# Leaky ReLU in one ScalarE instruction, state @ w_in in half-height matmuls, and conversions paced by a budget

## Chip, cores and metric

The kernel runs on one core of a Trainium2 chip. The metric is the device time of one execution in microseconds. TensorE (PE) does the matmuls, ScalarE (ACT) and VectorE (DVE) the elementwise work, and the SP queue issues nearly all DMAs.

## What is computed

State attention, and behind it two feed-forward layers, all on float32 arrays:

```python
# x: (8, 8, 512, 64), state: (8, 8, 32, 64): batch, head, tokens or states, depth
scores = scale * x @ state.T;  a = softmax(scores);   xread = a @ state
scores2 = scale * state @ x.T; a2 = softmax(scores2); sread = a2 @ x
x = concatenate([xread, sread], axis=2)         # then heads side by side: (4352, 512)
h = x @ w_in                                    # (512, 2048)
x = maximum(0.01 * h, h) @ w_out                # (2048, 512)
g, v = x @ w_gate, x @ w_val                    # (512, 1536) each
out = (g * sigmoid(g) * v) @ w_out2             # (1536, 512)
```

The five weights arrive as 64-bit floating-point numbers, seen by the kernel as pairs of 32-bit integers, and are turned into float32 on the chip.

## The kernel before, in words

**Precision.** A float32 matrix product is made of three passes of a faster format: each operand is split into a high part (a cast on ACT, `split_h`) and the rest (a subtraction on DVE, `split_l`), and `passes` multiplies low x high, high x low and high x high. Small products (scores, `state @ w_in`, the reads of the tokens) are plain float32 matmuls.

**First layer.** The tokens are worked on in 8 blocks of 512 (j = 0 to 7) and a tail of 256, which holds the results of the states. As `xread = a @ state`, the product `xread @ w_in` is taken as `a @ (state @ w_in)`: `state_win` multiplies the states of one batch and two pairs of heads with the raw w_in tiles, 64 output rows for each pair, and `store_sw` evicts the result from PSUM on ACT and stores it to DRAM (56 such products; those of batch 0 are kept in SBUF). They are loaded again (`load_sw`) when their block is due. For this the states lie in `states` with zeros around them, so that the two heads of a pair give rows of their own.

A block has 16 slots (f = 0 to 15, one for 128 columns of w_in). A slot i runs `h_mm` two slots ahead (6 matmuls of 512 columns), `h_act` (ACT copies PSUM to `hs`, DVE makes `max(0.01 hs, hs)`, ACT casts the high part, DVE subtracts for the low part) and `y_mm` (12 matmuls). The last block (j = 7) also does the tail: 12 + 12 matmuls of 256 columns in each slot.

**What sets the order.** The schedule is written out by hand, and every engine executes in program order. For the start and the first block it stands in strings, `START` and `SLOT0`: "c" is one step of the conversion of layer 1's weights, "p" one product of `state @ w_in` (nothing if none is ready), "H" `h_mm`, "Y" and "Z" `y_mm`, and so on. `put` places the attention steps of later blocks into slots by a cost and a budget of 2.8 per slot.

**Conversion.** `convert` is a generator that takes a weight tile through five operations on ACT and DVE, in four steps for each tile, with three tiles in different stages; `finish2` takes pairs of converted tiles of layer 2, makes sums of quarters (the second layer uses a product scheme with seven multiplications) and splits, and stores them to DRAM. In blocks 1 to 6, `pump` and `pump_finish` advance the two generators by one step in each slot, and by one more in every fourth; in block 7 by up to six and five steps. At slot f == Y_SUMS (6) of block 7 what is left is run to the end before anything else of the slot is issued (lines 1382 to 1393), and the memory is handed on to the second layer's weights. `read_tokens` (lines 361 to 424) makes the states' attention; `read` multiplies the turned weights with the tokens into 32 output rows for each head, and `read_out` turns the result in eight 32x32 transposes on DVE.

**Second layer.** Four pairs of blocks; for each the products with w_gate and w_val (`quads`, line 708) and then the product with w_out2 (`read_out`, line 829). Behind the third pair stands the tail (lines 859 to 960): for each of 12 column tiles f, `split2` splits a loaded gate and val tile and asks for the next load, `hidden` multiplies, and the result is multiplied with w_out2. All loads go through one list (`order`), three tiles of it ahead.

Of the kernel before, what the change touches and what calls it, by code (L numbers as in the profile page):

```python
# [25 lines left out]
def kernel(  # L26
# [54 lines left out]
    FB = 4  # L81
# [9 lines left out]
    START = "spc0Scppccc0pp0cppccppcc1pccchcc1cccpcp1clcppp0phcccpcplp1pc01cpcpmcc"  # L91
    SLOT0 = [
        "DcHcpAcccpcSYLpcpZccc",
        "DcHcAcccppSYLpccpZccc",
        "DcHcpcpcAcSYLZccppp",
        "cpDccHcApSpccYLpcZcccc",
        "cpDcHccAppScYLcZpc",
        "cccDpHpccApccScpYLccZ",
        "cpcDcHAcpScccYcLZpcp",
        "ccDccHcAppSccppYcLcZ",  # L100
        "pcDcHcpcAppSYLcccZ",
        "ccpDHcAScYcpLpccZcp",
        "ccpDcHcASYcpLpccZcp",
        "pcDHccASccYLcpcZp",
        "pcDHccASccYLcppcZp",
        "cpcDcHAccSpYLccpccpZp",
        "pDcpcHccpcppAcSYLcpZp",
        "ppDpcHccppAcSYLpcZp",
# [4 lines left out]
    Y_SUMS = 6  # L113
# [4 lines left out]
    PUMPS = [1, 1, 1, 1, 1, 1, 1]  # L118
    BUDGET = 2.8
    EARLY = -5  # L120
    BUDGET0 = 2.6
# [37 lines left out]
    sw_dram = [[dram.tile([2, P, 512], F32, name=f"sw_dram{b}_{g}") for g in range(FB)] for b in range(B)]  # L159
# [71 lines left out]
    def convert(keys, room, prepare, load_next, finish=None):  # L231

        done, before, prev = None, None, None
        for key in keys + [None, None]:
            while key and not room(key):
                yield 0
            ops = None
# [9 lines left out]
            yield 1  # L247
# [3 lines left out]
            yield 1  # L251
            if prev:
                prev["join"]()
            yield 1
# [9 lines left out]
            yield 1  # L264
# [9 lines left out]
    def pump_finish(n):  # L274
        for _ in range(n):
            next(finishing[0], None)
# [84 lines left out]
    def read_tokens(b, q):  # L361
# [32 lines left out]
        def read():  # L394

            ps = v["ps"] = ps_a.tile([P, 512], F32, tag="b", name="ps_r")
            tokens = [xn.pop((b, p)) for p in pairs]
            for c in range(NC):
                for j in range(4):
                    nc.tensor.matmul(  # L400
                        ps[NS * j:NS * (j + 1), 0:D],
                        lhsT=v["et"][:, c * P + NS * j:c * P + NS * (j + 1)],
                        rhs=tokens[j // 2][:, c, D * (j % 2):D * (j % 2 + 1)],
                        start=(c == 0),
                        stop=(c == NC - 1),
                    )
            next_xn(2)

        def read_out():
            for j in range(4):  # L410
                for g in range(2):
                    d0 = D * (j % 2) + 32 * g
                    nc.vector.transpose(
                        out=x_tail[d0:d0 + 32, pairs[j // 2], b * NS:(b + 1) * NS],
                        in_=v["ps"][NS * j:NS * (j + 1), 32 * g:32 * g + 32],
                    )
# [6 lines left out]
            {"D": [read_out], "cost": 0.9},  # L423
# [17 lines left out]
    sw_staged = [0]  # L441
# [10 lines left out]
    def store_sw(b, g, q, ps):  # L452

        pool, tag, bufs = ((cv, "sw", 2), (xin, "xn", 2))[sw_staged[0] % 2]
        sw_staged[0] += 1
        t = pool.tile([P, 512], F32, tag=tag, name="sw", bufs=bufs)
        nc.scalar.copy(t, ps)
        nc.sync.dma_start(out=sw_dram[b][g][q], in_=t)
# [13 lines left out]
    def load_sw(b, g, q):  # L472
        assert (g, b, q) not in products
        t = SW_raw[b, g, q] = xin.tile([P, 512], F32, tag="sw", name="sw")
        nc.sync.dma_start(out=t, in_=sw_dram[b][g][q])
# [30 lines left out]
    def h_act(j, f):  # L506
# [8 lines left out]
        nc.scalar.copy(hs, ps[:, :n])  # L515
# [175 lines left out]
    def layer2(p2, ps2):  # L691
# [167 lines left out]
        def tail():  # L859
# [5 lines left out]
            def load2():  # L865
                key = next(loads, None)
                if not key:
                    return
# [18 lines left out]
            for _ in range(3):  # L887
                load2()
# [564 lines left out]
```

## Time and profile before

| | us |
|---|---|
| median of 3 runs | 1517.83 (1517.43 to 1518.1) |
| the profiled execution | 1516.83 |
| its span, first to last instruction | 1515.0 |
| PE busy in it | 1460.5 |
| DVE busy | 944.6 |
| ACT busy | 683.4 |

The rows below come from the profile of one execution. A group of instructions is given as line, engine, operation, output <- inputs, shape and count, then the busy time in us, the mean of one in ns, and the idle time of its engine ahead of it with what ended that. A row of the timeline gives start, length, engine, line and tiles, a count, and in brackets the idle time before it. A row by stretches gives from and to, the length, the busy time of PE, PE's weight loads (PEld), DVE, ACT and POOL with the instructions counted, the mean granted clock of PE (1.00 is 2.4 GHz, 0.50 is 1.2 GHz), the busy share of the DMA engines and GB/s.

### The profile page before, as it was taken

What the parts mean: (1) busy time and instruction counts of PE and PEld (TensorE: products, weight loads), DVE (VectorE), ACT (ScalarE), POOL (GpSimd) and SP (SyncE); (2) the same over time, 40 slices, a digit from 0 to 9 for tenths busy, and PEclk for the clock granted to TensorE, in tenths of its full rate; (3) what the DMA queues carried; (4) which work ended last, traced back from release to release, by engine and by line L of the source; (5) the groups of instructions that cost most, each with busy time, mean ns of one, the idle gap of its engine ahead of it and who ended that gap; (6) DMA issues with size and microseconds to landing.
All of it is one profiled execution on the core that took longest, in us unless ns stands there. A gap on an engine that the chain in (4) does not pass through costs nothing.

```text
span 1515.0 us, 20085 instructions
## 1 busy us (share of the span) xinstructions
PE 1460.5 (96%) x7114; PEld 1157.6 (76%) x7114; DVE 944.6 (62%) x1716; ACT 683.4 (45%) x1234; POOL 3.0 (0%) x8
## 2 busy tenths in 40 slices
PE   6999999999999999919999999999999998999999
PEld 2446777777777788818888888888888887988887
DVE  6888688887887876976444544445344554544442
ACT  6777555565555555645433333334333342433322
POOL 0000000000000000000000000000000000000000
PEclk9999999999999999959999999999999998999999
DMA  8885444444454545785568677676766387786445
GB/s 296 294 282 198 140 157 177 153 174 157 164 194 161 188 137 183 262 271 183 162 193 274 205 235 229 194 221 228 235 200 194 105 285 230 225 279 192 130 141 193
DMA packets 146164, 307.53 MB, mean 203 GB/s; under 512 B 14608, under 2 KB 35088, under 8 KB 145040
## 3 DMA queue, kind: packets, MB, share of 16 engines
q1 hardware_dynamic: 144912, 297.85, 60.1%
q10 hardware_dynamic: 1152, 8.39, 1.3%
q8 instruction: 57, 0.93, 0.3%
q14 instruction: 43, 0.35, 0.1%
HBM read 231.74 MB, written 74.45 MB: 202 GB/s over the span
## 4 chain that ended last, share of the span: by engine, by line
PE 51%; DMA 4%; DVE 3%; ACT 1%; issue 0%; SPq 0%; ACTq 0%; DVEq 0%
PE ps_x L708 17%; PE ps_o L433 17%; PE ps_s L708 9%; PE ps_a L708 4%; DMA wraw<-w_val 2%; PE ps_y L433 1%; PE ps_h L433 1%; DMA ws<-in_dram 1%; PE ps_yt L433 1%; DMA wo<-wo 1%; PE ps_t L433 0%; DVE wl L165 0%; ACT wh L162 0%; DVE two L219 0%; DVE hl L165 0%
## 5 line engine op out<-in xcount | busy, mean ns | idle before, releaser
L433 PE MATMUL ps_y<-gh,w_parts 128*128 128x512 f32 x1024 | 339.0, 391 | 0.0
L708 PE MATMUL ps_x<-yc,wq 128*128 128x512 f32 x1152 | 278.0, 389 | 0.0
L708 PEld LDWEIGHTS ps_x<-yc,wq 128*128 128x128 f32 x1152 | 216.2, 188 | 44.8
L433 PE MATMUL ps_o<-wo,zh 128*128 128x512 f32 x768 | 236.5, 389 | 0.0
L433 PEld LDWEIGHTS ps_y<-gh,w_parts 128*128 128x128 f32 x1024 | 192.4, 188 | 52.0 <-issue 8.1
L433 PE MATMUL ps_y<-gl,w_parts 128*128 128x512 f32 x512 | 199.5, 390 | 0.2 <-DVE gl L165 0.2
L433 PEld LDWEIGHTS ps_o<-wo,zh 128*128 128x128 f32 x768 | 144.2, 188 | 30.0
L433 PE MATMUL ps_o<-wo,zl 128*128 128x512 f32 x384 | 149.5, 389 | 0.5 <-DMA wo<-wo 0.5
L708 PE MATMUL ps_s<-yc,wq 128*128 128x512 f32 x576 | 146.1, 389 | 0.0
L162 ACT CAST gh<-hs 128x512 fp32r<-128x512 f32 (+1 forms) x144 | 85.9, 596 | 118.1 <-DVE hs L516 118.1
L165 DVE TENSOR_TENSOR zl<-z,zh 128x512 fp32r<-128x512 f32 x96 | 66.3, 691 | 116.0 <-ACT zh L162 116.0
L165 DVE TENSOR_TENSOR gl<-hs,gh 128x512 fp32r<-128x512 f32 (+1 forms) x144 | 95.3, 662 | 56.9 <-ACT gh L162 54.0
L708 PEld LDWEIGHTS ps_s<-yc,wq 128*128 128x128 f32 x576 | 108.1, 188 | 22.4
L162 ACT CAST zh<-z 128x512 fp32r<-128x512 f32 x96 | 59.3, 622 | 142.1 <-PE ps_o L433 142.0
L728 ACT ACTIVATE sg<-C 128x512 f32<-128x512 f32 x72 | 45.5, 632 | 158.5 <-DVE C L724 158.5
L433 PEld LDWEIGHTS ps_y<-gl,w_parts 128*128 128x128 f32 x512 | 96.2, 188 | 20.1 <-DVE gl L165 0.5
L724 DVE TENSOR_TENSOR C<-ps_s,C 128x512 f32<-128x512 f32 x48 | 33.2, 691 | 124.2 <-PE ps_s L708 124.2
L516 DVE SCALAR_TENSOR_TENSOR hs<-hs 128x512 f32<-128x512 f32 (+1 forms) x144 | 94.5, 656 | 25.9 <-ACT hs L515 24.8
L515 ACT COPY hs<-ps_h 128x512 f32<-128x512 f32 (+1 forms) x144 | 80.5, 559 | 60.3 <-PE ps_h L433 58.5
L433 PE MATMUL ps_h<-ah,swl 128*128 128x512 f32 x256 | 106.4, 416 | 0.5 <-DVE swl L165 0.5
L433 PE MATMUL ps_h<-al,swh 128*128 128x512 f32 x256 | 100.6, 393 | 0.0
L433 PE MATMUL ps_h<-ah,swh 128*128 128x512 f32 x256 | 100.4, 392 | 0.0
(126 smaller groups left out, 2009.3 us busy)
## 6 DMA issues: line engine op xcount, KB each, us to landing
wo<-wo SPq DMA_DIRECT2D x96, 512.0 KB, 4.7
wq<-quad_gate SPq DMA_DIRECT2D x168, 256.0 KB, 3.1
wq<-quad_val SPq DMA_DIRECT2D x168, 256.0 KB, 3.1
ws<-in_dram SPq DMA_DIRECT2D x68, 512.0 KB, 4.6
sw_dram<-sw SPq DMA_DIRECT2D x56, 256.0 KB, 3.1
sw<-sw_dram SPq DMA_DIRECT2D x56, 256.0 KB, 3.8
quad_gate<-hl SPq DMA_DIRECT2D x24, 512.0 KB, 3.5
quad_val<-hl SPq DMA_DIRECT2D x24, 512.0 KB, 3.4
```

Source lines behind the costliest of these rows:

```text
L162: nc.scalar.copy(dst, src)
L165: nc.vector.tensor_tensor(out=dst, in0=src, in1=hi.bitcast(F32), op=ALU.subtract)
L433: nc.tensor.matmul(ps, lhsT=w, rhs=v, start=first and n == 0, stop=last and n == len(todo) - 1)
L515: nc.scalar.copy(hs, ps[:, :n])
L516: nc.vector.scalar_tensor_tensor(out=hs, in0=hs, scalar=0.01, in1=hs, op0=ALU.mult, op1=ALU.max)
L708: nc.tensor.matmul(bank, lhsT=a, rhs=v, start=first and n == 0, stop=last and n == len(todo) - 1, skip_group_check=True,)
L724: nc.vector.tensor_tensor(out=kept[0], in0=bank, in1=kept[0], op=ALU.add)
L728: nc.scalar.activation(t[0], c, AF.Sigmoid)
```

## The change

- `h_act`: one ACT instruction, `Prelu` with alpha 0.01, reads PSUM and writes `hs`; the DVE instruction is gone.
- `state @ w_in`: `product_sw` takes one pair of heads and four batches. Each head is a matmul with 64 contraction rows (the head's depth), 4 x 32 = 128 output rows and 512 columns, its operands on its own half of the partitions and its result in a PSUM bank of its own. There are 32 such products (batch 0 is in them too), each with two evictions on ACT and two stores. `load_sw` gathers a batch's rows from them. `flat` becomes a buffer of its own. `START` and `SLOT0` have fewer "p".
- `read`: the tokens become the stationary operand and the turned weights the moving one, so that the result arrives already turned; `read_out` is one copy.
- Conversions: every step yields a cost in us, and `fill` advances both generators until a credit is used up. In blocks 1 to 6 a slot gives `min(FILL, SLOT - CHUNK - load)`, in two halves; in block 7 slots before Y_SUMS give 2.0. `convert` goes on with tiles under way when there is no room for a new one. Y_SUMS is 5, and the y sums of the first pair are paced by slot.
- The tail of layer 2: the first two gate and val tiles and the first two w_out2 tiles are loaded at its first step, and each is replaced by the one two further on.

```diff
-    Y_SUMS = 6
+    Y_SUMS = 5
-    PUMPS = [1, 1, 1, 1, 1, 1, 1]
     BUDGET = 2.8
+    BUDGET0 = 2.6
+    FILL = 1.9
+    CHUNK = 0.8
+    SLOT = 4.1
...
+        todo = list(keys)
+        while todo or before or (finish and done):
+            key = todo.pop(0) if todo and room(todo[0]) else None
+            if not (key or before or (finish and done)):
                 yield 0
+                continue
...
+    def fill(us):
+        credit[0] = min(credit[0] + us, 2.0)
+        while credit[0] > 0:
+            cost = (next(finishing[0], None) or 0) + (next(background[0], None) or 0)
+            if not cost:
+                break
+            credit[0] -= cost
...
-            for c in range(NC):
-                for j in range(4):
-                    nc.tensor.matmul(
-                        ps[NS * j:NS * (j + 1), 0:D],
-                        lhsT=v["et"][:, c * P + NS * j:c * P + NS * (j + 1)],
-                        rhs=tokens[j // 2][:, c, D * (j % 2):D * (j % 2 + 1)],
...
+            for i in range(2):
+                for c in range(NC):
+                    for e in range(2):
+                        n = c * P + NS * (2 * i + e)
+                        nc.tensor.matmul(
+                            ps[D * e:D * (e + 1), i],
+                            lhsT=tokens[i][:, c, D * e:D * (e + 1)],
+                            rhs=v["et"][:, n:n + NS],
...
-            for j in range(4):
-                for g in range(2):
-                    d0 = D * (j % 2) + 32 * g
-                    nc.vector.transpose(
...
+            nc.vector.tensor_copy(out=x_tail[:, pairs[0]:pairs[0] + 2, b * NS:(b + 1) * NS], in_=v["ps"])
...
+    def product_sw(g, p, bs, banks):
+        pool = ps_y if banks == "yy" else ps_a
+        ps = [pool.tile([P, 512], F32, tag=tag, name="ps_sw") for tag in banks]
+        for e in range(2):
+            half = slice(D * e, D * (e + 1))
+            nc.tensor.matmul(
+                ps[e], lhsT=flat[half, p, 4 * bs:4 * bs + 4, :].rearrange("d b n -> d (b n)"),
+                rhs=raw["in", g, p][half], start=True, stop=True,
+            )
+        for e in range(2):
+            pool, tag, bufs = ((cv, "sw", 2), (xin, "xn", 2))[e]
+            t = pool.tile([P, 512], F32, tag=tag, name="sw", bufs=bufs)
+            nc.scalar.copy(t, ps[e])
+            nc.sync.dma_start(out=sw_dram[bs][g][2 * p + e], in_=t)
...
-        nc.scalar.copy(hs, ps[:, :n])
-        nc.vector.scalar_tensor_tensor(out=hs, in0=hs, scalar=0.01, in1=hs, op0=ALU.mult, op1=ALU.max)
+        nc.scalar.activation(hs, ps[:, :n], AF.Prelu, alpha=0.01)
...
-            for _ in range(3):
-                load2()
+            for f in range(2):
+                for kind in ("gate", "val"):
+                    load2(kind, f)
+            for f in range(2):
+                load2("o", f)
...
-                pump(PUMPS[0])
+                room = min(FILL, SLOT - CHUNK - load.get(i, 0))
+                fill(room / 2)
                 next(parts)
-                pump_finish(1)
                 y_mm(j, f)
-                pump(f % 4 == 2)
-                pump_finish(f % 4 == 0)
+                fill(room / 2)
...
                 if f < Y_SUMS:
-                    pump_finish(5)
+                    fill(2.0)
                 elif f == Y_SUMS:
-                    while next(background[0], None) is not None or next(finishing[0], None) is not None:
-                        pump(1)
-                        pump_finish(1)
+                    drain()
...
-                    for _ in range(2):
+                    while summed[0] < min(2 * (f - Y_SUMS), f):
                         next(sums0, None)
+                        summed[0] += 1
```

## Rows read from the trace of the kernel before

**Rows 1.** The page: busy time of the engines, and PE's line of 40 slices

```profile
PE 1460.5 (96%) x7114; PEld 1157.6 (76%) x7114; DVE 944.6 (62%) x1716; ACT 683.4 (45%) x1234; POOL 3.0 (0%) x8
...
PE   6999999999999999919999999999999998999999
```

**Rows 2.** PE's waits, whole span: us in total, times, longest

```profile
PE ps_h L433 <- DVE cl L165: 32.1, 1, 32.1
...
PE ps_t L433 <- DVE wl L165: 4.9, 2, 3.0
```

**Rows 3.** Timeline of PE around 650 us, three slots and the wait

```profile
636.25 0.28 PE L433 MATMUL ps_yt<-gh,w_parts 128*128 128x256 f32 x1
...
643.23 0.28 PE L433 MATMUL ps_yt<-gh,w_parts 128*128 128x256 f32 x1
...
676.90 0.55 PE L433 MATMUL ps_h<-tailh,cl 128*128 128x256 f32 x1 [32.08 <-DVE cl L165]
...
684.96 0.28 PE L433 MATMUL ps_yt<-gh,w_parts 128*128 128x256 f32 x1
```

**Rows 4.** Busy time by stretches: first block, blocks 1 to 6, hole, tail

```profile
36.00:134.70 98.70, 97.96 (x397) 47.03 (x396) 79.66 (x149) 75.81 (x138) 0.00 (x0) 1.00 0.83 285
158.50:589.80 431.30, 431.01 (x2380) 341.76 (x2379) 348.84 (x722) 237.51 (x437) 0.53 (x1) 1.00 0.47 161
...
644.80:677.00 32.20, 0.12 (x2) 0.13 (x1) 24.47 (x46) 15.28 (x27) 0.00 (x0) 0.55 0.81 285
...
1270.40:1331.60 61.20, 55.94 (x362) 51.01 (x361) 30.65 (x60) 22.68 (x49) 0.00 (x0) 0.92 0.76 240
```

**Rows 5.** Groups of instructions in 645 to 677 us, one of sixteen

```profile
L211 ACT ACTIVATE ws<-ws 128x512 f32<-128x512 f32 x7 | 4.6, 657 | 12.1 <-DMA ws<-in_dram 12.1
```

**Rows 6.** Groups over the whole span: elementwise work, table loads

```profile
L516 DVE SCALAR_TENSOR_TENSOR hs<-hs 128x512 f32<-128x512 f32 x128 | 87.8, 686 | 22.2 <-ACT hs L515 21.1
...
L515 ACT COPY hs<-ps_h 128x512 f32<-128x512 f32 x128 | 74.7, 583 | 55.7 <-PE ps_h L433 54.0 <-ACT yst L556 1.2
...
L413 DVE STREAM_TRANSPOSE x_tail<-ps_r 32x32 f32<-32x32 f32 x128 | 27.2, 213 | 1.8
...
L728 ACT ACTIVATE sg<-ps_x 128x512 f32<-128x512 f32 x24 | 14.3, 597 | 24.7 <-PE ps_x L708 24.7
...
L1199 ACT ACT_TABLE_LOAD x1 | 1.3, 1283 | 5.3 <-DMA flat<-in_dram 5.3
L728 ACT ACT_TABLE_LOAD x1 | 1.3, 1283 | 0.0
```

**Rows 7.** Groups of the first block, 36 to 134.7 us: the products

```profile
L446 PE MATMUL ps_sw<-w_in,states 128*64 128x512 f32 x192 | 47.9, 607 | 0.2 <-ACT sw L457 0.2
...
L457 ACT COPY sw<-ps_sw 128x512 f32<-128x512 f32 x42 | 24.4, 585 | 11.1 <-PE ps_sw L446 5.3 <-issue 2.4 <-DMA sw_dram<-sw 1.1
...
L446 PEld LDWEIGHTS ps_sw<-w_in,states 128*64 128x64 f32 x192 | 11.8, 135 | 24.3 <-issue 14.0 <-ACT sw L457 5.4 <-ACT ws L211 1.8
```

**Rows 8.** Timeline of PE and PEld: two products between other matmuls; weight loads

```profile
31.27 0.14 PEld L446 LDWEIGHTS ps_sw<-w_in,states 128*64 128x64 f32 x2 [0.29 <-issue]
...
38.36 0.39 PE L433 MATMUL ps_h<-ah,swh 128*128 128x512 f32 x1
38.67 1.94 PE L446 MATMUL ps_sw<-w_in,states 128*64 128x512 f32 x8
...
40.54 0.50 PE L433 MATMUL ps_y<-gh,w_parts 128*128 128x512 f32 x1
```

**Rows 9.** Timeline of PE: one read of the tokens

```profile
177.17 0.65 PE L400 MATMUL ps_r<-xn,et 128*32 128x64 f32 x32
```

**Rows 10.** Timeline of PE in layer 2's tail, one step to the next

```profile
1293.55 0.40 PE L433 MATMUL ps_o<-wh,zl 128*128 128x512 f32 x1
...
1297.81 0.40 PE L433 MATMUL ps_o<-wh,zl 128*128 128x512 f32 x1
```

**Rows 11.** The chain that ended last: start, us, what was on it

```profile
1273.38 6.32 DMA wraw<-w_val
```

More of the change, by code (lines that the diff above doesn't have):

```diff
@@ L157 @@
     wo_dram = [dram.tile([P, 2, 2, 512], F32, name=f"wo_{f}") for f in range(HF)]
-    sw_dram = [[dram.tile([2, P, 512], F32, name=f"sw_dram{b}_{g}") for g in range(FB)] for b in range(B)]
+    sw_dram = [[dram.tile([H, P, 512], F32, name=f"sw_dram{bs}_{g}") for g in range(FB)] for bs in range(B // 4)]
     def split_h(dst, src):
@@ L272, in pump @@
             next(background[0], None)
-    def pump_finish(n):
-        for _ in range(n):
-            next(finishing[0], None)
+    credit = [0.0]
+    def fill(us):
[5 more added lines that the diff above has]
+            credit[0] -= cost
     def pump_until(key):
@@ L450, in state_win @@
         return ps
[L452 to L458, printed above, removed]
+    def product_sw(g, p, bs, banks):
[6 more added lines that the diff above has]
+                rhs=raw["in", g, p][half], start=True, stop=True,
+            )
+        for e in range(2):
[3 more added lines that the diff above has]
+            nc.sync.dma_start(out=sw_dram[bs][g][2 * p + e], in_=t)
     def sw_tiles(b, g, q):
@@ L472, in load_sw @@
     def load_sw(b, g, q):
-        assert (g, b, q) not in products
+        assert not any((g, p, b // 4) in products for p in (2 * q, 2 * q + 1))
         t = SW_raw[b, g, q] = xin.tile([P, 512], F32, tag="sw", name="sw")
-        nc.sync.dma_start(out=t, in_=sw_dram[b][g][q])
+        rows = slice(NS * (b % 4), NS * (b % 4 + 1))
+        nc.sync.dma_start(
+            out=t, in_=sw_dram[b // 4][g][4 * q:4 * q + 4, rows]
+        )
     def split_sw_h(b, g, q):
@@ L860, in tail, with load2 @@
             n = widths[B]
-            order = [(key, f) for f in range(NF2) for key in ("gate", "val", "o")]
-            loads = iter(order)
             raw2, parts2 = {}, {}
-            def load2():
-                key = next(loads, None)
-                if not key:
+            def load2(kind, f):
+                if f >= NF2:
                     return
-                kind, f = key
                 if kind == "o":
@@ L875, in load2 @@
                         nc.sync.dma_start(out=t.bitcast(F32), in_=wo_dram[f // 2][:, f % 2, m])
[L876 removed]
+                    parts2[kind, f] = (h, l), (ht, lt)
                 else:
[L878 to L879 removed]
+                    raw2[kind, f] = wtiles[0].take("wraw")
+                    nc.sync.dma_start(out=raw2[kind, f][0], in_=w2_dram[kind, f % HF][:, f // HF])
             yr = []
@@ L937, in tail @@
             split2("val", 1)
-            split2("o", 0)
             yield
@@ L1017, in finish1_h @@
         def finish1_h(key):
-            while any((KD * g + 2 * q) // 2 + NF1 // 2 == key[1] for g, _, q in products):
+            while any((KD * g + p) // 2 + NF1 // 2 == key[1] for g, p, _ in products):
                 pump_products(1)
@@ L1274, in take0, with drain @@
             return t, None
+        summed = [0]
         preparing, after = ExitStack(), ExitStack()
+        def drain():
+            while True:
+                steps = [next(g[0], None) for g in (finishing, background)]
+                if steps == [None, None]:
+                    return
         turn_over = max(before["state"][-1], before["tokens"][-1]) + 1
```

115 lines of the change are left out of this document (47 added, 68 removed).

## Prediction

> **What bounds the kernel now.** I read the page's table of busy time first: TensorE (PE) is busy 96% of the span, VectorE (DVE) 62% and ScalarE (ACT) 45% [rows 1]. The row of slices shows one hole in PE's line, the "1" at the eighteenth slice, around 650 us, and a "6" at the start. So PE sets the pace nearly everywhere, and what can be won is either matmul time on PE or one of its few waits. The table of PE's waits names them: 32.1 us, once, for a DVE result in the tail's h_mm, and 4.9 us, twice, in the second layer's tail [rows 2]. The timeline around the first shows what it costs in all. In the last block (j = 7) the tail's first y matmul of a slot comes every 6.98 us; over the slot with the wait the distance is 41.73 us, so the price is 34.75 us: 32.08 us of waiting and 2.7 us in which PE, then at a granted clock of about 0.5, runs half as fast [rows 3, 4]. The groups of instructions inside the hole say who is late: the integer weights of the second layer are still being converted on DVE and ACT (the drain at f == Y_SUMS, lines 1383 to 1385), in program order ahead of the operand PE waits for, and ACT itself sits 12.1 us for loads of them [rows 5]. In the long stretch of blocks 1 to 6 PE is busy 431.01 of 431.30 us, DVE 348.8, ACT 237.5: PE-bound, with room on the others [rows 4]. In the first block's weight-loading stretch, 36 to 134.7 us, PE is busy 97.96 of 98.70 us, but DVE 79.7, ACT 75.8 and the DMA engines 0.83 of it too [rows 4]: the tightest place of the kernel.
>
> **The drain.** This is the largest term. Today blocks 1 to 6 give each slot one step of conversion and one of finishing, plus a quarter more, whatever the slot's other load. After, each slot gives `min(1.9, 3.3 - load)` us, in costs that are those of DVE's instructions. One weight tile costs 2.22 us to convert; the 36 of them and the last step are about 82 us. Finishing costs 12 x 4.54 + 6 x 1.48 = 63.4. Together 146. Adding the room slot by slot from the planner's own costs gives 161 us in slots 16 to 111, so the work should end near slot 104, before block 7 (slot 112) begins, and the drain, now one slot earlier, finds nothing. What hides the 146 us there is DVE's and ACT's free time, 82 and 194 us, and what the change frees. It frees, on DVE, 96 scalar_tensor_tensor of 686 ns (65.9 us), since ACT does the leaky ReLU as it empties PSUM, and 16 times eight transposes of 213 ns against one copy of about 0.2 us (24 us) [rows 6]. It brings in what the drain and the slots ahead of it do now: 24.5 us of DVE in the hole and at most 66 steps of about 0.55 us before it, 61 us. So DVE goes from 348.8 to at most 320 of 431 us, 74%. ACT pays nothing to speak of: an ACTIVATE from PSUM takes 597 ns, the copy it replaces 583 [rows 6]. Saved: 34.75 us. If a third of the work were left at the drain, a third of the price would stay.
>
> The second layer's weight loads and the y sums also start a slot earlier; they had ten slots and more before, and no PE wait in [rows 2] is theirs. Nothing.
>
> **The products state @ w_in.** Today 56 products of two matmuls each (two heads, 64 output rows each, one batch), of which 42 lie in the stretch 36 to 134.7, with 6 kept ones of the same form: 192 PE records busy 47.9 us, so four records, one product, take 1.00 us, the block's start included; the 42 evictions to store them are of 585 ns [rows 7]. The timeline gives the same: two products between a matmul at 38.36 and one at 40.54, 2.18 us less 0.23 for the first matmul itself, 0.97 each [rows 8] (0.23: a slot of 6.98 us in rows 3 holds 18 matmuls of 512 columns and 24 of 256, so 30 lengths of 512). After, 32 products of two matmuls with 64 contraction rows and 128 output rows; following the order of pumps through the code, 7 fall in the start phase (12 before) and 25 in this stretch. The form is not in this trace. Lower bound: the two run side by side as the two column halves do now (two weight loads in the 0.14 us of one [rows 8]), 1.00 us: 17 us of PE saved. Upper bound: one after the other, some 0.93 us more each (half of the 1.87 us from 38.67 to 40.54 [rows 8]), 25 x 1.93 = 48 against 42: 6 us lost. I take the lower one, because its nearest row is the same array shared by two matmuls, only cut the other way.
>
> The Trainium skill (TensorE: Matmul & The Clock Gate, section Measured speedup vs the span model) gives four row tiles 3.07 times the speed of one, not four. By that share, 0.77, a product would take about 0.28 us more, an estimate from that page, and 25 of them would put the forecast some 7 us higher; no run here shows row tiles yet.
>
> What is late next? ACT's work there stays (50 evictions for 25 products, 42 before: 75.8 + 4.7 = 80 us at most; DVE loses 12 x 0.686, to 71 us). DMA writes 50 x 256 KB for 42: 0.83 x 98.7 = 82 us, some 5 more. So PE's 98.7 - 17 = 82 us meets three others at 71 to 87. I take 12 of the 17 us, since DMA at 87 us is the highest of the four sums, and keep 4 and 18 as ends (18: the start phase, too, has five products fewer).
>
> **The reads of the tokens.** Turned round: 16 per call still, but with 64-column weights and 32 columns streamed, where now one read's 32 records take 0.65 us [rows 9]. Lower bound: half the streaming, -0.2 us. Upper: the weight loads set the pace, 11.8 us for 192 of 64 columns [rows 7], 0.061 us each, 32 of them 1.97 us: +1.3. Nearer the row of the read itself, where loads hide: +0.2 us, 16 times, 3 us lost in a PE-bound stretch; ends -3 and +21.
>
> **The tail of layer 2.** The stretch 1270.4 to 1331.6 takes 61.2 us at a mean granted clock of 0.92 [rows 4]; a steady step of it takes 4.26 us [rows 10], twelve 51.1. (Such a step has six matmuls of 512 columns, 1.4 us, and 24 of 256, 2.9.) The 10.1 us between are the two waits and the half clock behind them: the gate and val tiles of f = 1 are asked for only when those of f = 0 are split, on SP behind the loads of `wo`; the val tile's load, issued at 1273.38, takes 6.32 us to land [rows 11]. After, f = 0 and 1 are loaded at the first step of the tail, far earlier, beside the y sums of the fourth pair, and the same late places fetch f = 2. That is wanted a step later: 1270.4 + 5.8 for the gate and val of f = 0 and 1 + 1.4 for the first output + 1.4 for the gate of f = 2 = 1279.0, against 1273.4 + 6.3 + 1.4 for its split = 1281.1 at worst. So a wait of 0 to 2 us may stay. 9 us saved, ends 5 and 10.
>
> **Sum.** The profiled execution took 1516.83 us (span 1515.0): 1516.83 - 34.75 - 12 - 9 + 3 = 1464.1. It lies 1.0 us under the median of the runs shown, 1517.83, so I forecast 1465.
>
> **The rivals.**
> The first block gives little back: DMA and the in-order ACT queue, both near 0.8 already [rows 4], keep the 98.7 us stretch at 94 or so. For: all four sums come within 15% of each other. Against: no PE wait there is put down to a load [rows 2]. 8 us less saved: 1473.
> The two 64-row matmuls run one after the other: no gain but 6 us lost in the first block, 18 more than forecast: 1483.
> Part of the drain stays: fill steps return nothing while a load is under way, and ACT's 12.1 us of waiting for loads [rows 5] shows that loads can set the pace. With a third left: 1477.
> Prelu does not share a table with Exp. The trace has two table loads of 1.283 us [rows 6], one of them before the first copies, and none between the Exps and the copies. Two more around each of 32 Exps would be 82 us of ACT, mostly in its free time in blocks 1 to 6, but 5 us of it on the path of the start: 1470. The Trainium skill (ScalarE: Activation LUTs, Rules for kernel authors) puts relu and max on VectorE rather than ScalarE; the float32 rows here speak otherwise, 686 ns on DVE against about 597 on ACT.
> Slower: the fills make DVE the bound of blocks 1 to 6. A filled slot holds 4.0 us of DVE by the budget (3.3 and the low half of g), against 431.3 / 96 = 4.49 us of PE. In the hole, conversions kept DVE busy only 24.5 of 32.2 us [rows 4], 1.31 us of time for each of work; if that held in the filled slots, they would take 5.2 us, and 88 of them 0.75 us more each, 66 us: 1531. It decides from 5.1 us a slot on. Against: in the hole ACT waited for loads, and DVE's mean afterwards is 74%.
>
> **How the numbers follow.** Chances: the forecast (with its ends, 1453 to 1469) 0.53; first block gives little 0.18; serial row tiles 0.11; part of the drain stays 0.10; table loads 0.03; slower 0.04; the change does not do what it says, since the slots fill no better and the products gain nothing, 0.01. The range leaves out the last three and the far ends: 1453 to 1483. A measurement of this kernel tells about 0.2%, 3 us, from no change: faster 0.95, same 0.01, slower 0.04.
>
> **What would show it.** Right: no PE wait for `cl` near 640 us, slots of 6.98 us throughout block 7, blocks 1 to 6 at 431 us or little more, the last conversion before block 7; groups of products of about 1.0 us; no wait on `wl` beyond 2 us in the tail, and a granted clock of 1.00 there. Wrong: PE waits for gl or swl in blocks 1 to 6 (the fills), products of 1.9 us (serial tiles), ACT waiting for `ws` loads in the first 130 us (DMA). The forecast itself falls if the hole moves rather than closes.

## The result, and the profile after

The changed kernel takes 1481.15 us (median of four runs, 1480.25 to 1482.51) against 1517.63 for the kernel before: a ratio of 0.9765, 95% interval 0.9748 to 0.9782. That is 36.5 us less, inside the predicted range of 1453 to 1483, but 16 us above the 1465 that was forecast and above the ends of the forecast itself, 1453 to 1469. The profiled execution took 1480.25 us, with a span of 1478.2.

Cut by stage, the spans (1515.0 and 1478.2) compare as follows. A block ends where ACT begins to copy its result out of PSUM (`yst<-ps_y`).

| stage | before, us | after, us | difference | forecast |
|---|---|---|---|---|
| start and first block (0 to the end of block 0) | 158.45 | 155.35 | -3.1 | -12 |
| blocks 1 to 6 | 431.30 | 438.28 | +7.0 | +3 |
| block 7, with the drain | 138.05 | 103.76 | -34.3 | -34.75 |
| second layer | 787.2 | 780.8 | -6.4 | -9 |

So the largest term came out to half a microsecond; the first block and the tail gave less than their share, and the reads, which make up the second row, cost more than theirs.

The page after: busy time of the engines and PE's line of slices.

```profile
PE 1450.5 (98%) x7018; PEld 1159.7 (78%) x7018; DVE 829.4 (56%) x1460; ACT 688.2 (47%) x1242; POOL 3.0 (0%) x8
...
PE   5999999999999999999999999999999999999998
```

The hole of [rows 1] is gone and only the start and the last slice are below 9. DVE has lost 115 us of work, and its last conversion of a weight ends at 588 us, before block 7 begins at 593.63; before the change it was at 675, inside block 7. The waits of PE, whole span (us in total, times, longest):

```profile
PE ps_s L319 <- ACT states L1213: 7.0, 1, 7.0
PE ps_sw L467 <- DVE w_in L225: 5.5, 1, 5.5
PE ps_sw L467 <- ACT sw L475: 5.2, 6, 1.2
PE ps_o L443 <- DMA wo<-wo: 2.0, 1, 2.0
PE ps_sw L467 <- DVE swl L168: 1.4, 2, 0.8
PE ps_h L443 <- DVE swl L168: 1.0, 2, 0.5
PE ps_t L443 <- DVE wl L168: 0.9, 1, 0.9
```

The 32.1 us for `cl` of [rows 2] are not among them, and `wl` has fallen from 4.9 to 0.9. Three have grown: the products wait for ACT to evict them (L475, six times), one wait is for a load of `wo`, and one is for the first converted tile of w_in. Before the change they were these:

```profile
PE ps_sw L446 <- DVE w_in L222: 2.5, 4, 1.4
PE ps_o L433 <- DMA wo<-wo: 0.5, 1, 0.5
PE ps_sw L446 <- ACT sw L457: 0.2, 1, 0.2
```

Busy time by stretches (from and to, length, PE, PEld, DVE, ACT, POOL with counts, granted clock, DMA share, GB/s); the first is the stretch of the first block that answers to the first row of [rows 4], then blocks 1 to 6, block 7, and layer 2's tail:

```profile
36.00:131.00 95.00, 89.63 (x327) 47.77 (x328) 76.21 (x144) 78.65 (x146) 0.00 (x0) 0.99 0.90 307
155.35:593.63 438.28, 438.28 (x2379) 350.48 (x2378) 306.43 (x604) 266.99 (x486) 0.53 (x1) 1.00 0.60 206
593.63:697.40 103.77, 103.77 (x624) 92.90 (x623) 39.55 (x68) 46.60 (x94) 0.00 (x0) 1.00 0.33 106
1234.00:1296.00 62.00, 60.92 (x400) 55.37 (x399) 34.39 (x65) 24.33 (x53) 0.00 (x0) 1.00 0.81 266
```

Block 7 has no idle PE at all, at a granted clock of 1.00, and DVE is 70% busy in blocks 1 to 6. In the first block, though, PE idles 5.4 us of 95.0 where it idled 0.74 of 98.7 before: what was taken from PE there was only partly time won. The groups of instructions say what the new forms cost (mean ns after the busy time; then idle time and what ended it):

```profile
L536 ACT ACTIVATE hs<-ps_h 128x512 f32<-128x512 f32 x128 | 76.6, 599 | 133.7 <-PE ps_h L443 132.5 <-DVE r L352 0.5 <-DVE st L353 0.5
L467 PE MATMUL ps_sw<-w_in,flat 64*128 64x512 f32 x128 | 43.8, 656 | 12.1 <-DVE w_in L225 5.5 <-ACT sw L475 5.2 <-DVE swl L168 1.4
L475 ACT COPY sw<-ps_sw 128x512 f32<-128x512 f32 x64 | 35.0, 590 | 11.8 <-PE ps_sw L467 6.6 <-DMA sw_dram<-sw 3.1 <-PE ps_sw L455 1.3
```

`Prelu` takes 599 ns, the copy it replaced 583 [rows 6], and there are still only two table loads. The timeline of PE around one product (start, us, line, tiles, count):

```profile
40.81 0.39 PE L443 MATMUL ps_h<-ah,swh 128*128 128x512 f32 x1
41.13 1.13 PE L467 MATMUL ps_sw<-w_in,flat 64*128 64x512 f32 x4
42.19 0.50 PE L443 MATMUL ps_y<-gh,w_parts 128*128 128x512 f32 x1
```

From 40.81 to 42.19 are 1.38 us, less 0.23 for the first matmul: 1.15 us for the product. The same reading of [rows 8] gave 0.97 each for two products in a row. One after the other the two heads would have taken some 1.9. They do run side by side.

### The profile page after: what moved, and what is told of

Read it like the earlier page. It is cut to its first block, busy times and chain, and to the rows that moved or that the text cites. A ratio compares the mean times of both kernels' runs of the same rounds, so it can differ in the third digit from the quotient of the medians.

```text
span 1478.2 us, 19617 instructions
## 1 busy us (share of the span) xinstructions
PE 1450.5 (98%) x7018; PEld 1159.7 (78%) x7018; DVE 829.4 (56%) x1460; ACT 688.2 (47%) x1242; POOL 3.0 (0%) x8
## 4 chain that ended last, share of the span: by engine, by line
PE 93%; DMA 3%; ACT 2%; DVE 1%; issue 1%; SPq 0%; ACTq 0%; DVEq 0%
PE ps_y L443 23%; PE ps_o L443 18%; PE ps_x L728 18%; PE ps_h L443 14%; PE ps_s L728 9%; PE ps_a L728 4%; PE ps_t L443 2%; PE ps_yt L443 2%; PE ps_sw L467 2%; PE ps_r L416 1%; PE ps_s L319 1%; DMA wo<-wo 1%; DMA wraw<-w_gate 1%; DMA sw_dram<-sw 1%; ACT sw L475 1%
## 5 line engine op out<-in xcount | busy, mean ns | idle before, releaser
L536 ACT ACTIVATE hs<-ps_h 128x512 f32<-128x512 f32 (+1 forms) x144 | 82.7, 575 | 180.2 <-PE ps_h L443 179.0
L740 ACT COPY C<-ps_x 128x512 f32<-128x512 f32 x96 | 56.1, 584 | 94.6 <-PE ps_x L728 93.8
```

The costliest lines, as they stand in the source:

```text
L536: nc.scalar.activation(hs, ps[:, :n], AF.Prelu, alpha=0.01)
L740: nc.scalar.copy(t[0], src)
```

## The experiments

All kernels below are the changed kernel with one edit, unless said otherwise, each compared with the kernel before in the same runs (1516.2 to 1517.0 us there).

### The drain: pacing, and a loop that goes on

The old pacing, one step of each generator per slot and a quarter more (every entry of `PUMPS` is 1); the drain and the y sums at slot 6:

```diff
-                fill(room / 2)
+                pump(PUMPS[0])
                 next(parts)
+                pump_finish(1)
                 y_mm(j, f)
-                fill(room / 2)
+                pump(f % 4 == 2)
+                pump_finish(f % 4 == 0)
...
-                    fill(2.0)
+                    pump_finish(5)
```

> The changed kernel with conversions advanced as before, one step of each kind per slot and a quarter more, the drain and the y sums at slot 6; all other changes stay. Theory that the fills alone close the hole: a PE wait of about 32 us for cl returns in block 7, which takes 136 to 139 us for 103.8, blocks 1 to 6 stay at 436 to 438, in all 1510 to 1516. Rival that the DVE time freed by Prelu and by the turned reads already lets the conversions run ahead, so that the hole would close without the fills: steps are counted, not timed, yet a hole of under 20 us would speak for it, 1490 to 1502.

Measured: 1504.41 us, ratio 0.9916 (0.9896 to 0.9936); block 7 takes 123.1 us. The wait came back, but at 13 us, not 32. That is neither time that was expected; a hole of under 20 us was to speak for the rival, the freed DVE time. The changed generator has a second new feature: when there is no room for a new tile it goes on with those under way, where the old loop stood still. A further kernel undoes that as well:

```diff
-        todo = list(keys)
-        while todo or before or (finish and done):
-            key = todo.pop(0) if todo and room(todo[0]) else None
-            if not (key or before or (finish and done)):
+        for key in keys + [None, None]:
+            while key and not room(key):
                 yield 0
-                continue
```

> The changed kernel with the old pacing (one step of each kind per slot and a quarter more) and with the old loop of the generator as well, which stands still while there is no room for a new tile; all else stays changed. With the old pacing alone the wait for cl was 13.0 us and block 7 took 123.1 us (103.8 in the changed kernel, 138.1 before). Theory that the loop that goes on with tiles under way is the other part of the gain: the wait for cl comes back to 25 to 32 us, block 7 takes 133 to 138, 1513 to 1518 in all. Rival that the DVE time freed by Prelu and the reads is that part: block 7 stays at 121 to 126, 1502 to 1506.

Measured: 1515.22 us, ratio 0.9995 (0.9985 to 1.0005); block 7 takes 136.2 us. PE's longest wait with the old pacing, and with the old loop as well:

```profile
PE ps_h L448 <- DVE cl L169: 13.0, 2, 12.7
```

```profile
PE ps_h L445 <- DVE cl L169: 30.4, 2, 30.1
```

So the theory holds: of the 32.5 us between 136.2 and 103.8, the pacing (with the drain and the y sums a slot earlier) is worth 19.3, and the loop, under the old pacing, 13.2. The old loop under the new pacing was not run. The second kernel has `Prelu` and the turned reads too, and its wait is 30.4 us: the DVE time that they free did not close the hole by itself. With the drain back, the kernel is no faster than before: this term carries the whole gain, and what all other edits give and take nets to about nothing.

### The reads of the tokens as before

```diff
-                            ps[D * e:D * (e + 1), i],
-                            lhsT=tokens[i][:, c, D * e:D * (e + 1)],
-                            rhs=v["et"][:, n:n + NS],
+                        ps[NS * j:NS * (j + 1), 0:D],
+                        lhsT=v["et"][:, c * P + NS * j:c * P + NS * (j + 1)],
+                        rhs=tokens[j // 2][:, c, D * (j % 2):D * (j % 2 + 1)],
```

> The changed kernel with the reads of the tokens as before (32 output rows for each head, eight transposes). Theory: a turned read takes 1.13 us of PE against 0.65, 16 times, in a stretch that PE bounds, so this kernel is 7.6 us faster: 1473.5, blocks 1 to 6 in 431 us. Rival: the eight transposes and their planner cost of 0.9 slow the fills down, so that conversions run into block 7 and part of the gain goes back: 1476 to 1485.

Measured: 1476.72 us, ratio 0.9737 (0.9721 to 0.9753). One read in the changed kernel on PE, with its weight loads, and one in this kernel:

```profile
174.83 1.13 PE L416 MATMUL ps_r<-et,xn 128*64 128x32 f32 x32
...
174.83 1.01 PEld L416 LDWEIGHTS ps_r<-et,xn 128*64 128x64 f32 x32 [0.35 <-ACT gh L165]
```

```profile
174.19 0.65 PE L414 MATMUL ps_r<-xn,et 128*32 128x64 f32 x32
...
154.71:585.44 430.73, 430.73 (x2379) 342.07 (x2378) 330.01 (x715) 266.44 (x486) 0.53 (x1) 1.00 0.60 207
```

Blocks 1 to 6 take 430.73 us instead of 438.28. The turned read is 0.48 us longer, 16 times 7.7 us, which is the whole loss of those blocks, and the weight loads fill 1.01 of its 1.13 us. I read this as the loads setting the pace: half the streamed columns saved nothing, twice the stationary columns cost all of it. It was not tested alone, for the old form also has four results of 32 rows beside each other in the array and the new one two of 64. The Trainium skill (TensorE: Matmul & The Clock Gate, Step-by-step: what each phase is for) says that a load's time goes with the number of stationary columns; the loads agree, 0.49 us for 32 of 32 columns in the trace of before and 1.01 for 32 of 64 in that of the changed kernel. DVE takes on 24 us of transposes again (330.0 for 306.4). The last conversion now ends some 6 us into block 7, as the rival had it, but block 7 still takes 103.76 us: nothing waits for it. The whole kernel gains less than the blocks: its second layer took 784.3 us in this profile, 3.5 more than that of the changed kernel, with the same code.

### The products as before

```diff
-        for e in range(2):
-            half = slice(D * e, D * (e + 1))
-            nc.tensor.matmul(
-                ps[e], lhsT=flat[half, p, 4 * bs:4 * bs + 4, :].rearrange("d b n -> d (b n)"),
-                rhs=raw["in", g, p][half], start=True, stop=True,
-            )
...
+    def store_sw(b, g, q, ps):
...
+                    store_sw(b, g, q, state_win(b, g, q, banks[bank[0] % len(banks)]))
```

`START` and `SLOT0` are those of before too.

> The changed kernel with the products as they were before (56 products of two heads' 64 output rows, old order of pumps), all else as changed. Accounting of the two traces: the first block ends only 3.1 us earlier than before, though 17 us of PE time were taken out of it. If the products gave those 3 us and no more, this kernel takes about 1484 (3 us over the changed kernel's 1481), and its first block ends near 158. If Prelu and the other parts have slowed the first block and the products gave 12 or more, it takes 1490 or more. If the products cost time as they are now placed, it takes less than 1480.

Measured: 1483.91 us, ratio 0.9779 (0.9765 to 0.9794), whose interval overlaps that of the changed kernel. In the profiles it is 3.9 us longer, but 3.2 of them lie in the second layer (784.0 us for 780.8), whose code is the same. The first block ends at 156.09 us instead of 155.35. That is no difference: the kernels with the old pacing and with the old tail have the first block of the changed kernel, and end it at 156.72 and 156.50. And of the 3.1 us that the block gained on the kernel before, 2.4 are there with the old products too.

Two changes of opposite sign lie in that. With the old products the first y matmul starts at 39.88 us, with the new ones at 42.19 (41.78 and 42.01 in the two kernels just named); from there to the block's end it is 116.2 and 113.2 us (114.9 and 114.5). So the new products bought 1.3 to 3.05 us in the slots, and 1.9 to 2.3 went back at the start, where PE waits 5.5 us for its first tile of w_in (2.1 with the old products, which wait 2.4 for a load of `xt` besides) and, after three more waits, runs its first `h_mm` at a granted clock of 0.50 (from 35 to 38.3 us).

The slots of the first block, first y matmul to block end, by stretch and by the groups of the products; the kernel before, then the changed one:

```profile
40.54:158.45 117.91, 117.17 (x482) 62.93 (x481) 95.35 (x176) 85.27 (x155) 0.00 (x0) 1.00 0.74 254
...
L446 PE MATMUL ps_sw<-w_in,states 128*64 128x512 f32 x194 | 48.5, 607 | 0.2 <-ACT sw L457 0.2
...
42.19:155.35 113.16, 107.13 (x406) 60.91 (x405) 85.13 (x160) 86.72 (x162) 0.00 (x0) 1.00 0.82 276
...
L467 PE MATMUL ps_sw<-w_in,flat 64*128 64x512 f32 x98 | 31.3, 640 | 4.3 <-ACT sw L475 4.3
L455 PE MATMUL ps_sw<-w_in,states 128*64 128x512 f32 x24 | 7.2, 618 | 0.0
```

PE's busy time falls by 10.0 us, all of it in the products (48.5 to 38.5), and its idle time rises by 5.3, from 0.74 to 6.03.

### What takes the freed time of the first block

Three kernels with one suspect each, then two with several together. The stores left out (loads read tokens in their place), and the evictions reading a weight tile in SBUF so that no PSUM bank waits for ACT:

```diff
-            nc.sync.dma_start(out=sw_dram[bs][g][2 * p + e], in_=t)
```

> The changed kernel without the 64 stores of the products (16.8 MB); the 56 later loads read an input of the same size instead of them, so that part of the result is left out. Evictions stay. DMA theory: the first block is paced by the DMA engines (0.90 of them busy, 307 GB/s), and with a third of its traffic gone its end comes 6 to 9 us earlier, total 1472 to 1475. PSUM theory: the products wait for the two evictions of the product before, which stand in ACT's queue; without stores nothing of that changes but the 3 us in which ACT waits for a staging buffer: 1478 to 1481, and PE's wait for sw stays at 5 us or so.

```diff
-            nc.scalar.copy(t, ps[e])
+            nc.scalar.copy(t, raw["in", g, p])
```

> The changed kernel with the 64 evictions reading the raw w_in tile in SBUF instead of the product in PSUM: same work on ACT, same stores, but no matmul waits for an eviction (the products' values are left out of the result). PSUM theory: PE's waits for sw (5.2 us, and 15.4 us of its weight loads) go, and the first block ends 5 to 9 us earlier: 1472 to 1476. DMA theory: no change within 2 us, 1479 to 1483. If neither this nor the kernel without stores gains, ACT and DVE in program order set the pace.

Two operations of layer 1's conversion left out, the low words on ACT and their addition on DVE:

```diff
-                ops["low"]()
+                if not finish:
+                    ops["low"]()
...
-                prev["add"]()
+                if not finish:
+                    prev["add"]()
```

> The changed kernel without two of the operations in the conversion of the first layer's weights, the low words on ACT (0.68 us) and their addition on DVE (0.69 us): 64 instructions less in all between the start and the end of the first block, some 22 us of ACT and 22 of DVE; the last three bits of the converted weights are left out. Theory that ACT and DVE in program order set the pace of the first block once its matmuls are fewer (78.7 and 76.2 us of 95 there): the first block ends 3 to 8 us before 155.35, and the PE waits for w_in and sw shrink; 1472 to 1478. Rival that loads of the weights or PE itself set it: its end moves by under 1 us, 1479.5 to 1481.5.

Without the stores and those two operations; then all three edits at once:

> The changed kernel without the low words and their addition in the conversion of the first layer's weights, and without the 64 stores of the products, whose loads read tokens instead (results are not those of the reference). Each alone left the first block's end where it was, within 2.1 us (156.4 and 153.2, against 155.35). Theory that two limits lie side by side there, the conversions on ACT and DVE and the stores, behind which ACT waits for a free buffer of the evictions: without both the first block ends at 143 to 149, in all 1468 to 1475. Rival that PE's own work in program order with ACT and DVE of the same slot sets it: it ends at 151 to 154 and the PE waits for sw stay at 4 us or more.

> As the kernel without the low words, their addition and the stores, and in addition the evictions of the products read a weight tile in SBUF in place of PSUM, so that no PSUM bank waits for ACT (results are not those of the reference). Theory of several limits side by side: the first block ends 1 to 4 us earlier than without the conversions' two operations and the stores alone, at 141 to 147. Rival that PE's matmuls themselves are the bound by then: no earlier by more than 1 us.

Measured:

| kernel | us | first y, at | block 0 ends | from one to the other |
|---|---|---|---|---|
| before | 1517.63 | 40.54 | 158.45 | 117.9 |
| changed | 1481.15 | 42.19 | 155.35 | 113.2 |
| no stores | 1480.33 | 40.98 | 153.23 | 112.3 |
| evictions from SBUF | 1479.30 | 42.86 | 153.16 | 110.3 |
| less conversion | 1481.86 | 41.04 | 156.41 | 115.4 |
| less conversion, no stores | 1476.38 | 38.33 | 148.75 | 110.4 |
| all three | 1469.65 | 39.89 | 144.19 | 104.3 |

The theory for "less conversion" fell: ACT has some 17 us and DVE 19 less to do in the first block, and it ends 1 us later. The last column varies by up to 1.8 us among kernels with one and the same first block (113.2, 114.5 and 114.9, above), so the 0.9 and the -2.2 of single edits can hardly be told from nothing, the less as the profile of "less conversion" is that of the slowest of its four runs (1484.24); the 2.9 of the evictions is clear of it, though 5 to 9 were expected of the block's end and 2.2 came. No single one of the suspects is the bound. Together they are: all three take 8.9 us out of the slots, more than the single ones do in sum, and with two and with three edits the block ends in the ranges that were expected (148.75 and 144.19). What is left there is PE:

```profile
39.89:144.19 104.30, 102.93 (x406) 58.89 (x405) 68.81 (x133) 73.39 (x136) 0.00 (x0) 1.00 0.55 172
...
L469 PE MATMUL ps_sw<-w_in,flat 64*128 64x512 f32 x98 | 27.9, 640 | 0.3
L457 PE MATMUL ps_sw<-w_in,states 128*64 128x512 f32 x24 | 6.5, 618 | 0.0
```

PE is busy 102.93 of 104.30 us, the products take 34.4 us for the 48.5 of the kernel before, and the slots are 13.6 us shorter than there. So the time taken from PE does come back as soon as the others keep up. The order of ACT in the changed kernel shows how they hang together:

```profile
109.89 0.59 ACT L165 CAST swh<-ps_sw 128x512 fp32r<-128x512 f32 x1 [2.08 <-PE ps_sw L455]
...
113.00 1.21 ACT L475 COPY sw<-ps_sw 128x512 f32<-128x512 f32 x2 [0.90 <-DMA sw_dram<-sw]
114.11 0.63 ACT L344 ACTIVATE st<-st 128x512 f32<-128x512 f32 x1
116.26 1.21 ACT L475 COPY sw<-ps_sw 128x512 f32<-128x512 f32 x2 [1.51 <-DMA sw_dram<-sw]
117.37 0.62 ACT L165 CAST gh<-hs 128x512 fp32r<-128x512 f32 x1
```

ACT waits 2.1 us for PE, then 0.9 and 1.5 us until an earlier store has left the buffer that an eviction is to fill; meanwhile PE waits for that eviction:

```profile
111.33 1.13 PE L467 MATMUL ps_sw<-w_in,flat 64*128 64x512 f32 x4
113.64 1.75 PE L467 MATMUL ps_sw<-w_in,flat 64*128 64x512 f32 x4 [1.18 <-ACT sw L475]
```

With the stores gone PE still waits 0.72 us at this place, and 0.67 to 0.90 for evictions at others. With the conversions cut the eviction stands behind a store for longer, 1.75 us: in that kernel the waits of ACT for `sw_dram<-sw` grew from 3.1 to 5.0 us. Without the need to evict (all three) PE's waits for `sw` are gone:

```profile
PE ps_s L321 <- ACT states L1211: 7.2, 1, 7.2
PE ps_sw L469 <- DVE w_in L222: 4.2, 1, 4.2
PE ps_h L445 <- DVE al L168: 4.2, 1, 4.2
PE ps_o L445 <- DMA wo<-wo: 2.6, 2, 2.3
```

Less conversion alone also loses to the clock: PE waits 1.96 us for an eviction, and from 113 to 119 us it runs at a granted clock of 0.50 to 0.55. At the same place kernels with the same first block differ: with the old tail the granted clock is 0.66 from 115 to 120 us, in the changed kernel it stays at 1.00.

```profile
115.00:120.00 5.00, 5.00 (x16) 3.44 (x16) 2.58 (x6) 3.37 (x6) 0.00 (x0) 0.66 1.02 313
...
115.00:120.00 5.00, 5.00 (x20) 3.01 (x20) 1.98 (x5) 3.70 (x7) 0.00 (x0) 1.00 0.99 325
```

That this is the whole of the 2.2 us of less conversion was not tried.

### The leaky ReLU as before

```diff
-        nc.scalar.activation(hs, ps[:, :n], AF.Prelu, alpha=0.01)
+        nc.scalar.copy(hs, ps[:, :n])
+        nc.vector.scalar_tensor_tensor(out=hs, in0=hs, scalar=0.01, in1=hs, op0=ALU.mult, op1=ALU.max)
```

> The changed kernel with the leaky ReLU as before: ACT copies PSUM to hs, DVE makes max(0.01 hs, hs) in place. Everything else stays changed, so blocks 1 to 6 hold the fills and 96 DVE instructions of 0.686 us more: DVE there 306.4 + 65.9 = 372 of 438 us, 85%. Theory that Prelu mainly frees DVE, which has room without it: blocks 1 to 6 stay within 2 us of 438.3, the first block ends 1 to 3 us later than 155.35 (DVE is busy 76.2 of 95 us there and takes on 9 to 10 more instructions), in all 1482 to 1486. Rival that Prelu is what makes the fills affordable: a filled slot would hold 4.0 + 0.7 = 4.7 us of DVE against 4.5 of PE, blocks 1 to 6 become 10 to 30 us longer with PE waits for gl or swl, 1492 to 1512.

Measured: 1491.84 us, ratio 0.9835 (0.9814 to 0.9855), between the two expectations. Blocks 1 to 6 and a part of the first block:

```profile
162.93:605.59 442.66, 439.82 (x2384) 350.90 (x2383) 365.73 (x701) 265.63 (x486) 0.53 (x1) 1.00 0.59 203
110.00:131.00 21.00, 19.09 (x61) 10.37 (x59) 12.33 (x23) 12.12 (x23) 0.00 (x0) 0.84 0.71 240
```

With 59 us more of DVE, blocks 1 to 6 lose 4.4 us, all in the last two of them (1.7 and 2.7), so the fills are affordable either way, with little to spare. The surprise is the first block: it ends at 162.93 us, 7.6 later than in the changed kernel and 6.2 to 6.4 later than in the two kernels with the same first block. There the instruction lies in the chain from PE over ACT and DVE back to PE, and 21 us at a mean granted clock of 0.84 come with it. It is also 4.5 us later than in the kernel before, which has the old leaky ReLU and the old products; with the old products `Prelu` goes with 2.4 us (158.45 to 156.09). So in these profiles the new products cost the first block time where `Prelu` is missing. `Prelu` is thus worth 10.7 us in the changed kernel, of which the forecast had none as a term of its own.

### The tail of the second layer as before

```diff
-            for f in range(2):
-                for kind in ("gate", "val"):
-                    load2(kind, f)
-            for f in range(2):
-                load2("o", f)
+            for _ in range(3):
+                load2()
```

> The changed kernel with the loads of the second layer's tail as before, one list with three tiles ahead. Theory that the early loads are worth the waits in the tail: waits on wl of about 5 us and the half clock behind them come back, the tail takes 60 to 61 us for 53.2, and the wait of 2.0 us for wo behind the eight early loads goes, so 5 to 7 us more in all: 1486 to 1488. Rival that the early loads cost elsewhere what they give in the tail: 1480 to 1482.

Measured: 1488.69 us, ratio 0.9814 (0.9792 to 0.9835), 7.5 us above the changed kernel, a little more than expected. Its longest sum of PE waits:

```profile
PE ps_t L443 <- DVE wl L168: 7.0, 4, 3.8
```

The second layer takes 787.6 us against 780.8 in the changed kernel. The other kernels here with the tail of the changed one took 780.8 to 784.5 for it, so the early loads are worth 3 to 7 us. All of these have a wait that the kernel of this section doesn't have, for a load of `wo`, of 0.6 to 3.8 us; it is not all that differs among them, for the shortest of these waits don't go with the shortest second layers. In the changed kernel it is this row:

```profile
1192.42 0.47 PE L443 MATMUL ps_o<-wo,zl 128*128 128x512 f32 x1 [1.96 <-DMA wo<-wo]
```

The same wait sums to 3.2 us with the old products and to 3.8 with less conversion. It comes 7 us after the first step of the tail, where now eight loads are issued at once (1180.9 to 1185.5 us).

### A version that is faster than both

The reads as before, and the two w_out2 tiles of the tail asked for one step later each:

```diff
-            for f in range(2):
-                load2("o", f)
...
                 split2(kind, 0)
+                load2("o", 0 if kind == "gate" else 1)
                 yield
```

> The changed kernel with the reads of the tokens as before, and with the first two w_out2 tiles of the second layer's tail asked for one per step, behind the splits of the gate and val tiles of f = 0, not at the first step of the tail. Theory: blocks 1 to 6 take 430.7 us as with the old reads alone (438.3 in the changed kernel), and the PE waits for wo, 2.0 to 3.0 us behind the eight early loads, go to under 1: 1471 to 1475. Rival that those waits come from the load of the DMA engines and not from the order of the queue: they stay, 1476 to 1478.

Measured: 1474.60 us, ratio 0.9726 (0.9710 to 0.9742), just clear of the changed kernel's interval. The wait for `wo` fell to 1.0 us, but the one for `wl` rose to 2.6. Against the kernel with the old reads alone (0.9737) the second edit can't be told from nothing; the old reads make the version. That two of the eight early loads come later goes with a shorter wait for `wo`, but two kernels with all eight, evictions from SBUF and less conversion without stores, show 0.6 and 0.8 us. So whether the wait is behind those loads in the queue, or comes from the load of the DMA engines as the rival has it, stays open.

## Why the forecast held, and where it was off

**The drain** was right in place and size: 34.3 of 34.75 us. No wait for `cl`, no half clock, no idle PE in block 7. That the work would fit was argued from DVE's sum over blocks 1 to 6, at most 320 us; it was 306. The margin was thinner than reckoned: the work was to end near slot 104 and ended at 588 us, some six slots later and 5 us before block 7. But the prediction gave all of it to the budget per slot. The change of the generator's loop, which stood in its diff, gave 13 of it under the old pacing.

**The first block** is the step that failed: 12 us (4 to 18) were forecast, 3.1 came, and 2.4 of them came with the old products too. The products themselves were priced well: 1.0 us taken, 1.15 measured. In the slots their records fell from 48.5 to 38.5 us, and by 14 where evictions don't hold them up. What failed was the next sentence, that the time then falls to the highest of four sums. Sums of busy time bound a stretch only if each engine can work ahead; here they take turns in program order. Eight products that show 1.27 to 1.81 us instead of 1.13 hide 3.6 us, PE's idle time rose by 5.3, and the slots gained 4.75, of which 1.65 were lost at the start. The rival "the first block gives little" named the place and was the one that came true. Its reason, the DMA engines and ACT's order near 0.8, was half of it: without the stores, with the DMA engines at 0.3 to 0.7, the slots still gained only 0.9.

**The reads** cost 7.6 us for the 3 forecast, within the ends given. The prediction set the upper price, weight loads at 0.061 us each, against the row of the read itself, where loads hide behind streaming, and took a value near the second. After the turn the loads fill 1.01 of 1.13 us, so they hide no more. Each took 0.032 us, half the upper price, which came from the loads of the products [rows 7].

**The tail** gave 6.4 for 9 (ends 5 and 10), and in the ten other kernels with the same tail 2.7 to 5.5, seven of them under the lower end. The mechanism was right: the granted clock is 1.00 and `wl` costs 0.9 us, within the "0 to 2 us" of the working. Missed was a wait for the `wo` of the products before: 2.0 us here, up to 3.8 elsewhere, and none in the kernel with the old tail. "Far earlier" put the loads among others with due times of their own.

**The number.** That 1481 lies inside the range is part luck. It is above the forecast's own ends, and the rival time nearest to it, 1483, is that of serial row tiles, which the trace refutes. It came about as three shortfalls of about 9, 4 and 3 us in one direction, where each rival had one.

**The other rivals.** Serial row tiles: refuted, 1.15 us per product and not 1.9. The estimate from the Trainium skill (TensorE: Matmul & The Clock Gate, Measured speedup vs the span model), a share of 0.77 taken from four row tiles, would have meant 1.28; the trace of these two row tiles, at 1.15, shows no loss of that size. Table loads: none. Part of the drain stays: none. Fills that make DVE the bound: not with `Prelu`, 306 of 438 us; with the old leaky ReLU the mechanism shows in two blocks, 4.4 us, where PE's longest wait, 2.2 us, is for ACT, which has itself just waited 2.16 us for `hs` from DVE.

## What to carry to other kernels

Before work is taken off the bounding engine, look at who hands it its buffers: where PE, ACT, DVE and the stores follow each other in one written order, matmul time turned into waits until the evictions could work ahead, and no engine's share of busy time showed that beforehand. Price a matmul of few streamed columns by its weight load too: here the form with fewer stationary columns was the faster one. Before a difference of a microsecond or two in one stage is given to an edit, look at kernels in which that stage was left alone: here they differ by 1.8 us in the first block's slots and by almost 4 in the second layer. And background work that must be done by a certain point is best given out by time and never allowed to stand still; that was worth more here than all the other edits together.

## What the hardware showed that was not expected

Two matmuls that share the array by rows cost next to nothing more than two that share it by columns, float32 at 512 columns. The products of batch 0 still have the old form (L455), and one stands in the same place between other matmuls:

```profile
90.26 0.39 PE L443 MATMUL ps_y<-gh,w_parts 128*128 128x512 f32 x1
90.58 1.08 PE L455 MATMUL ps_sw<-w_in,states 128*64 128x512 f32 x4
91.59 0.50 PE L443 MATMUL ps_h<-ah,swl 128*128 128x512 f32 x1
```

From 90.26 to 91.59 are 1.33 us, 1.10 without the first matmul, against 1.15 for two matmuls of 64 contraction rows, which give twice as many output rows. And in a run of small weight loads one of 32 columns takes 15 ns (0.49 us for 32), one of 64 takes 32 ns (1.01 for 32); the matmuls of 32 streamed columns with the latter come every 35 ns, close to the pace of their loads.
